# Attention's z and query scores as one product per head on 64x32 parts of TensorE's array

## The chip, the cores and the metric

The kernel runs on one core of one Trainium2 chip. The metric is the device time of one execution in microseconds (us), the median of several runs.

## The reference, cut to what matters

Two stages stand one behind the other: a "pack" attention over 8 batches of 8 heads, then two MLPs over all 4608 tokens.

```python
def sm_attn(qq, kk, vv):
    s = scale * np.matmul(qq, kk.transpose(0, 1, 3, 2))
    a = softmax(s)                       # max, exp, sum, divide
    return np.matmul(a, vv)
...
p_packed = sm_attn(p, k, v)              # 32 packed rows of 64 for each head; k, v have 576 rows
out = sm_attn(q, p_packed, p_packed)     # 576 query rows for each head
...
x = out.transpose(0, 2, 1, 3).reshape(4608, 512)
h = x @ w_in;   x = (h - tanh(h)) @ w_out            # first MLP, 512 -> 2048 -> 512
h = x @ w_in2;  x = (s * relu(h)**2 + b) @ w_out2    # second MLP, same sizes
```

The kernel never forms `out`. It multiplies the packed rows of each head with the head's 64 rows of `w_in` first, z = p_packed @ w_in (for each batch 8 heads x 32 rows by 2048 columns), and then h = z^T a2, where a2 are the 256 attention weights of a token (8 heads x 32).

## The kernel before

The program of all engines is written out in one order by hand. The main loop goes over the batches b, the two halves hf of a batch's 576 tokens (288 each), and 16 tiles j of 128 hidden columns. For each j it issues `mm1` (6 products of 128x288 into the PSUM tile `h`, L386), `act1` and `split_g` (tanh on ScalarE, the subtraction and the low part on VectorE, L394, L395, L131, L132), and `mm2` (12 products into four PSUM tiles `acc`, L409) for a tile two or three steps back.

Everything else is a generator, `fill`, that issues one small step at every call of `slot()`: `mm1` calls it once, each of `mm2`'s four groups of three products once, and the loop once more. So one step follows about three products of the main loop. `wait(n)` lets n steps pass. For each batch `fill` makes `step_p` and `stage1` (scores of p against k, softmax, product with v, the packed rows transposed into `pblk`), `make_z` for c = 0 to 3 (512 hidden columns each), and `second_stage` for the two halves, which is `stage2` (query scores, softmax, `a2`) for g = 0 and 1, four heads each, issued in turn by `both`. `more`, the conversion of the second MLP's weights through `cv` (L118 to L659), gets every third step.

A matrix `pblk[b][:, g]` holds four heads. Its 128 rows are (u, e, d): two halves u of the head dimension, two heads e of a pair, 32 dims d. Its 128 columns are the four heads' 32 packed rows. `mask` sets to zero the rows of the other head of a pair. So one product takes a pair of heads hp: contraction over all 128 rows, half of them zeros, 64 output partitions (the 64 columns of the pair):

```python
# pair_scores (L228): the query scores of group g, 288 tokens
nc.tensor.matmul(ps[hp*64:hp*64+64, :hi-lo], lhsT[:, hp*64:hp*64+64], kts[hp][:, lo:hi], ...)
# make_z (L362): z of group g, 512 hidden columns
nc.tensor.matmul(ps[g][hp*64:hp*64+64, :], pblk[b][:, g, hp*64:hp*64+64], w1[c][:, 2*g+hp, :], ...)
```

Both are float32 products; the profile has two matmul records for each of them. The trace writes their part of the array as 128\*64. `stage2` transposes a pair's q with VectorE (`qT`, L315), waits `W_Q` = 3 steps, issues the two products of its group, and VectorE transposes the scores back out of PSUM (L324). `make_z` puts group 0 and group 1 into two PSUM tiles `zp` one step apart, then ScalarE copies a tile into z (L366) and VectorE subtracts the copy for the low part (L368), group 0 first. `zp`, the score tiles and the other attention tiles share two PSUM banks (`bank_a`); `h` has two of its own (`bank_h`). SyncE issues the loads of k (L170, four transfers of 64 partitions for each group), q (L197) and w_in (L148).

Of the kernel before, what the change touches and what calls it, by code (L numbers as in the profile page):

```python
# [18 lines left out]
def pack_attention_two_mlps(ctx, tc, q, k, v, p, w_in1, w_out1, w_in2, w_out2, s_in, b_in, out):  # L19

# [51 lines left out]
    mask = apool.tile([P, 2, 2, D // 2], F32, name="mask")  # L72
# [67 lines left out]
    def load_w1(c, i):  # L140

        t = wslot(I64, f"w1s_{c}_{i}", [P, CH // 2, CW])
        rows = w_in1[i * 2 * P:(i + 1) * 2 * P, c * CW:(c + 1) * CW]
        rows = rows.rearrange("(t e u d) f -> u e d t f", e=2, u=2, d=32)
        for u in range(2):
            for e in range(2):
                p0 = (2 * u + e) * 32
                nc.sync.dma_start(out=t[p0:p0 + 32], in_=rows[u, e])  # L148
        return t
# [7 lines left out]
    k_t, v_t, q_t, pc_t, ppT, pblk, a2, z = {}, {}, {}, {}, {}, {}, {}, {}  # L157
# [3 lines left out]
    def load_k(b, g, slot=None):  # L161
        for hp in range(2):
            h0 = 4 * g + 2 * hp
            if slot is None:
                t = apool.tile([P, NB, 32], F32, tag="kr", name=f"k_{b}_{g}_{hp}", bufs=2)
            else:
                t = slot.rearrange("p a c -> p (a c)")[:, hp * S:(hp + 1) * S].rearrange("p (n m) -> p n m", m=32)
            for u in range(2):
                src = k[b, h0:h0 + 2, :, u * 32:u * 32 + 32].rearrange("e (r n) d -> (e r) n d", n=NB)
                nc.sync.dma_start(out=t[u * 64:u * 64 + 64], in_=src)  # L170
            k_t[b, g, hp] = t
# [16 lines left out]
    def load_q(b, hf):  # L188
        for g in range(G):
            for hp in range(2):  # L190
                h0 = 4 * g + 2 * hp
                t = apool.tile([P, HB // 32, 32], F32, tag="qr", name=f"q_{b}_{hf}_{g}_{hp}", bufs=4)
                for u in range(2):
                    for e in range(2):
                        src = q[b, h0 + e, hf * HB:(hf + 1) * HB, u * 32:u * 32 + 32]
                        p0 = (2 * u + e) * 32
                        nc.sync.dma_start(out=t[p0:p0 + 32], in_=src.rearrange("(n r) d -> r n d", r=32))  # L197
                q_t[b, hf, g, hp] = t
# [7 lines left out]
    def step_p(b):  # L206
        pc = pc_t.pop(b)
        pp = apool.tile([P, G, P], F32, tag="pp", name=f"pp_{b}")
        for g in range(G):
            nc.vector.tensor_tensor(  # L210
                out=pp[:, g].rearrange("p (u e d) -> p u e d", u=2, e=2),
                in0=pc[:, g].rearrange("p (u e d) -> p u e d", u=2, e=1).to_broadcast([P, 2, 2, D // 2]),
                in1=mask, op=ALU.mult)
        yield from wait(W_P)
        ps = bank_a(f"ppT_{b}")
        for g in range(G):
            nc.tensor.transpose(ps[:, g * P:(g + 1) * P], pp[:, g], ident)
        yield
        ppT[b] = apool.tile([P, G, P], F32, tag="ppT", name=f"ppT_{b}", bufs=2)
        nc.scalar.copy(ppT[b], ps[:, :G * P])  # L220
        yield
# [9 lines left out]
    def stage1(b, g, then_k=None, then_v=None, slot=None):  # L231
# [57 lines left out]
        for c in range(CT):  # L289
            n = P if c < C - CT else R  # L290
            for hp in range(2):
                nc.tensor.matmul(ps[hp * 64:hp * 64 + 64, :P], e1T[:n, c, hp * 64:hp * 64 + 64],  # L292
                                 vt[:n, 2 * hp:2 * hp + 2, c].rearrange("r e (u d) -> r u e d", u=2),
# [3 lines left out]
        if then_v:  # L297
            load_v(*then_v)
        pk = apool.tile([P, P], F32, tag="pk", name=f"pk_{b}_{g}", bufs=2)
        nc.vector.scalar_tensor_tensor(out=pk, in0=ps[:, :P], scalar=nm[:, 9:10],  # L300
                                       in1=mask.rearrange("p u e d -> p (u e d)"), op0=ALU.mult, op1=ALU.mult)
# [9 lines left out]
    def stage2(b, hf, g):  # L311
        qT = []
        for hp in range(2):
            qT.append(apool.tile([P, HB], F32, tag="qT", name=f"qT_{b}_{hf}_{g}_{hp}", bufs=4))
            nc.vector.transpose(out=qT[hp], in_=flat(q_t.pop((b, hf, g, hp))))  # L315
            yield
        yield from wait(W_Q)
        ps = bank_a(f"s2_{b}_{hf}_{g}")
        pair_scores(ps, pblk[b][:, g], qT, 0, HB)
        yield  # L320
        NBK = HB // 32
        t = apool.tile([P, NBK, M], F32, tag="t2", name=f"t2_{b}_{hf}_{g}", bufs=2)
        st = apool.tile([P, 3, NBK, 1], F32, tag="st", name=f"st_{b}_{hf}_{g}", bufs=2)
        nc.vector.transpose(out=flat(t), in_=ps[:, :HB])  # L324
        yield
# [29 lines left out]
    def make_z(b, c):  # L355
        zt = wpool.tile([P, 2, G, CW], F32R, tag="w", name=f"z_{b}_{c}")
        z[b, c] = zt
        ps = []
        for g in range(G):
            ps.append(bank_a(f"zp_{b}_{c}_{g}"))  # L360
            for hp in range(2):
                nc.tensor.matmul(ps[g][hp * 64:hp * 64 + 64, :], pblk[b][:, g, hp * 64:hp * 64 + 64],  # L362
                                 w1[c][:, 2 * g + hp, :], start=True, stop=True)
            yield
        for g in range(G):
            nc.scalar.copy(zt[:, 0, g], ps[g])  # L366
            yield
            nc.vector.tensor_tensor(out=zt[:, 1, g], in0=ps[g], in1=zt[:, 0, g].bitcast(F32), op=ALU.subtract)  # L368
            yield
# [91 lines left out]
    with tc.manual_schedule():  # L461
# [72 lines left out]
        def second_stage(b, hf):  # L534
            yield from both([stage2(b, hf, g) for g in range(G)])
            done.add(("a", b, hf))
# [39 lines left out]
        for h4 in range(4):  # L576
            nc.vector.memset(mask[h4 * M:(h4 + 1) * M, :, h4 % 2], 1.0)
# [31 lines left out]
        def second_weights():  # L609
# [23 lines left out]
            for n in range(N):  # L633
# [32 lines left out]
                if out2 and f == FT - 1:  # L666
                    ps = bank_a(f"cs_{i}")
                    for h in range(2):
                        nc.tensor.matmul(ps[:, 2 * h:2 * h + 2], csum[:, h], ones, start=True, stop=True)
                    yield  # L670
# [525 lines left out]
```

## Time and profile before

| what | value |
|---|---|
| median of 3 runs | 1614.13 us (1612.8 to 1617.1) |
| the profiled execution's own time | 1611.81 us |
| its span, first to last instruction | 1610.0 us |
| mean granted TensorE clock | 0.979 of 2.4 GHz |
| busy: TensorE, VectorE, ScalarE, GpSimd | 94%, 68%, 46%, 7% of the span |

The attention and the first MLP end at about 880 us, the second MLP fills the rest. Matmul records are pipelined: each lasts from its start to the end of its last column, so successive records overlap, and the price of a product is read from one start to the next. PEld is TensorE's weight load, DVE is VectorE, ACT is ScalarE, SPq is SyncE's queue.

### The profile page before, as it was taken

To read this page: it belongs to the slowest core of one execution; us is meant where nothing else is said; L and a number is where in the kernel's file an instruction comes from. 1 tells how busy PE (TensorE), PEld (TensorE's weight loads), DVE (VectorE), ACT (ScalarE), POOL (GpSimd) and SP (SyncE) were. 2 spreads that over 40 slices of the span, in tenths; PEclk is the share of its full clock that TensorE was granted. 3 is DMA by queue.
4 is the path that set the end of the run, shared out by engine and by line. 5 is a ranking of instruction groups with operands and counts; after the bars stand their busy time and mean duration, and the time that the engine had idled before them with its cause. 6 is when DMAs were issued, how large, how long until landed. Compare 5 with 4: busy or idle time off the path is not lost.

```text
span 1610.0 us, 26179 instructions
## 1 busy us (share of the span) xinstructions
PE 1514.9 (94%) x9592; PEld 1397.2 (87%) x9592; DVE 1091.7 (68%) x2076; ACT 745.9 (46%) x1417; POOL 109.7 (7%) x143
## 2 busy tenths in 40 slices
PE   5577999999999999999999999999998899999998
PEld 2466688888888888888799999999998899999998
DVE  5987676867768677686744677777664565565554
ACT  2344344444444444444433566566554554454452
POOL 0343100000000000000101000000011000000000
PEclk9798999999999999999999999999999999999999
DMA  9746554463544535354534754664689876786783
GB/s 193 184 107 155 124 136 117 112 153 87 140 116 124 135 100 145 97 130 111 155 116 154 295 212 181 238 244 169 228 316 396 308 224 193 225 238 183 222 256 79
DMA packets 395345, 285.65 MB, mean 177 GB/s; under 512 B 242640, under 2 KB 340944, under 8 KB 395216
## 3 DMA queue, kind: packets, MB, share of 16 engines
q1 hardware_dynamic: 386624, 254.03, 53.7%
q0 software_dynamic: 8064, 29.36, 5.0%
q8 instruction: 75, 1.23, 0.3%
q10 hardware_dynamic: 528, 0.59, 0.1%
q14 instruction: 54, 0.44, 0.1%
HBM read 168.43 MB, written 115.47 MB: 176 GB/s over the span
## 4 chain that ended last, share of the span: by engine, by line
PE 77%; DVE 10%; DMA 7%; issue 2%; SPq 2%; ACT 2%; ACTq 0%; POOL 0%; DVEq 0%; POOLq 0%
PE acc L409 20%; PE h L386 10%; PE Y L1136 9%; PE Y L921 8%; PE Z L1136 6%; PE X L1136 6%; PE X L921 5%; PE Z L921 5%; PE zp L362 3%; DMA g<-g 3%; PE s L228 2%; DMA w1s<-in_moe_w_in_dram 1%; PE pv L292 1%; DVE gl L132 1%; DVE t L395 1%
## 5 line engine op out<-in xcount | busy, mean ns | idle before, releaser
L409 PE MATMUL acc<-gh,wo 128*128 128x288 f32 x2040 | 423.2, 298 | 0.0
L409 PEld LDWEIGHTS acc<-gh,wo 128*128 128x128 f32 x2040 | 334.2, 191 | 0.0
L409 PE MATMUL acc<-gl,wo 128*128 128x288 f32 x1020 | 316.4, 310 | 5.9 <-POOL gl L132 5.5
L394 ACT ACTIVATE t<-h 128x288 f32<-128x288 f32 x256 | 105.4, 412 | 324.6 <-PE h L386 277.2
L409 PEld LDWEIGHTS acc<-gl,wo 128*128 128x128 f32 x1020 | 195.0, 191 | 55.7 <-issue 35.1
L395 DVE TENSOR_TENSOR t<-h,t 128x288 f32<-128x288 f32 x256 | 115.2, 450 | 184.7 <-ACT t L394 184.2
L386 PE MATMUL h<-a2h,z 128*128 128x288 f32 x1024 | 215.1, 298 | 3.2 <-DVE z L368 3.2
L836 DVE TENSOR_TENSOR x<-B,x 128x768 fp32r<-128x768 f32 x158 | 146.7, 950 | 87.8 <-ACT x L1070 72.4
L386 PE MATMUL h<-a2l,z 128*128 128x288 f32 x512 | 157.7, 308 | 20.6 <-DVE a2l L352 19.1
L386 PEld LDWEIGHTS h<-a2h,z 128*128 128x128 f32 x1024 | 166.3, 191 | 3.7 <-DVE z L368 3.7
L921 PE MATMUL Y<-x,w 128*128 128x384 f32 x864 | 161.1, 340 | 8.7 <-DVE g L836 7.9
L921 PEld LDWEIGHTS Y<-x,w 128*128 128x128 f32 x864 | 153.7, 191 | 9.3 <-DVE g L836 8.3
L1136 PE MATMUL Y<-x,w 128*128 128x384 f32 x864 | 153.2, 335 | 0.7 <-DVE s L836 0.7
L1136 PEld LDWEIGHTS Y<-x,w 128*128 128x128 f32 x864 | 150.3, 188 | 1.0 <-DVE s L836 1.0
L386 PEld LDWEIGHTS h<-a2l,z 128*128 128x128 f32 x512 | 97.9, 191 | 39.0 <-DVE a2l L352 20.6
L1070 ACT CAST x<-B 128x768 fp32r<-128x768 f32 x116 | 93.6, 833 | 51.0 <-DMA B<-g 30.3
L921 PE MATMUL Z<-x,w 128*128 128x384 f32 x576 | 109.9, 340 | 4.2 <-DVE u L836 4.2
L131 ACT CAST gh<-t 128x288 fp32r<-128x288 f32 x255 | 108.7, 426 | 1.1 <-DVE t L395 1.1
L921 PE MATMUL X<-x,w 128*128 128x384 f32 x576 | 108.1, 336 | 0.0
L921 PEld LDWEIGHTS Z<-x,w 128*128 128x128 f32 x576 | 102.4, 191 | 4.5 <-DVE u L836 4.5
L1136 PE MATMUL X<-x,w 128*128 128x384 f32 x576 | 102.2, 335 | 0.0
L132 DVE TENSOR_TENSOR gl<-t,gh 128x288 fp32r<-128x288 f32 x224 | 102.0, 456 | 0.0
(148 smaller groups left out, 2089.2 us busy)
## 6 DMA issues: line engine op xcount, KB each, us to landing
g<-g SPq DMA_DIRECT2D x196, 384.0 KB, 3.6
B<-g SPq DMA_DIRECT2D x116, 384.0 KB, 4.6
w<-w_d POOLq DMA_DIRECT2D x28, 512.0 KB, 6.7
w<-wo_d POOLq DMA_DIRECT2D x28, 512.0 KB, 8.0
k<-in_k_dram SPq DMA_DIRECT2D x64, 144.0 KB, 4.3
q<-in_q_dram SPq DMA_DIRECT2D x256, 36.0 KB, 2.1
B<-x2t SPq DMA_DIRECT2D x24, 384.0 KB, 5.7
g<-s SPq DMA_DIRECT2D x24, 384.0 KB, 2.6
```

The source lines that it names most:

```text
L131: nc.scalar.copy(hi, x)
L132: (eng or nc.vector).tensor_tensor(out=lo, in0=x, in1=hi.bitcast(F32), op=ALU.subtract)
L228: nc.tensor.matmul(ps[hp * 64:hp * 64 + 64, :hi - lo], lhsT[:, hp * 64:hp * 64 + 64], kts[hp][:, lo:hi], start=True, stop=True)
L362: nc.tensor.matmul(ps[g][hp * 64:hp * 64 + 64, :], pblk[b][:, g, hp * 64:hp * 64 + 64], w1[c][:, 2 * g + hp, :], start=True, stop=True)
L386: nc.tensor.matmul(h[:, :HB], zt[:, zi, g, f0:f0 + P], a[:, g], start=(n == 0), stop=(n == 3 * G - 1))
L394: nc.scalar.activation(t, h[:, :HB], AF.Tanh)
L395: nc.vector.tensor_tensor(out=t, in0=h[:, :HB], in1=t, op=ALU.subtract)
L409: nc.tensor.matmul(acc[m][:, :HB], w[:, m * P:(m + 1) * P], x, start=(j == js[0] and i == 0), stop=(j == js[-1] and i == 2))
L836: self.nc.vector.tensor_tensor(out=o, in0=a, in1=b, op=op)
L921: self.nc.tensor.matmul(bank[:, f, :self.TH], w[:, f, a, kt], x[:, b, kt], start=(p in ("P1", "P5", "P6") and m == 0), stop=(m == 5), skip ...
L1070: self.nc.scalar.copy(self.xs[(7 * self.NBK + n) % self.XS][:, 0], self.ready[0])
L1136: nc.tensor.matmul(bank[:, ft, :T], w[:, kk, u, ft], x[:, v, kk], start=first and p in ("P1", "P5", "P6"), stop=last, skip_group_check=True)
```

## The change

The rows of `pblk` are now (e, u, d) by pair: the even head of each pair has rows 0 to 63, the odd head rows 64 to 127, and q, k and w_in are loaded in that order. z and the query scores are made by one new function, `head_products`: one product per head, with contraction over its own 64 rows and 32 output partitions, so each takes a 64x32 part of the array. Head 2i+e goes to PSUM tile e, partitions 32i to 32i+31; all eight heads of a z or of a half's scores stand in succession. The new generator `scores2` transposes all four pairs of q, waits `W_Q` steps, and issues the eight products of both PSUM tiles; `stage2` begins behind that. A set `taken` makes a generator wait a step at a time until both tiles of the last user have been handed to VectorE. The mask is no longer applied to the packed rows (a `tensor_scalar` takes the place of a `scalar_tensor_tensor`), k is loaded in eight transfers of 32 partitions, and the small `cs` product of the second MLP's bias uses `bank_h`.

```diff
         t = wslot(I64, f"w1s_{c}_{i}", [P, CH // 2, CW])
-        rows = w_in1[i * 2 * P:(i + 1) * 2 * P, c * CW:(c + 1) * CW]
-        rows = rows.rearrange("(t e u d) f -> u e d t f", e=2, u=2, d=32)
-        for u in range(2):
-            for e in range(2):
-                p0 = (2 * u + e) * 32
-                nc.sync.dma_start(out=t[p0:p0 + 32], in_=rows[u, e])
+        rows = w_in1[i * 2 * P:(i + 1) * 2 * P, c * CW:(c + 1) * CW].rearrange("(t p) f -> p t f", p=P)
+        for r in range(4):
+            nc.sync.dma_start(out=t[r * 32:r * 32 + 32], in_=rows[r * 32:r * 32 + 32])
         return t
...
                 t = slot.rearrange("p a c -> p (a c)")[:, hp * S:(hp + 1) * S].rearrange("p (n m) -> p n m", m=32)
-            for u in range(2):
-                src = k[b, h0:h0 + 2, :, u * 32:u * 32 + 32].rearrange("e (r n) d -> (e r) n d", n=NB)
-                nc.sync.dma_start(out=t[u * 64:u * 64 + 64], in_=src)
+            for e in range(2):
+                for u in range(2):
+                    src = k[b, h0 + e, :, u * 32:u * 32 + 32].rearrange("(r n) d -> r n d", n=NB)
+                    p0 = (2 * e + u) * 32
+                    nc.sync.dma_start(out=t[p0:p0 + 32], in_=src)
             k_t[b, g, hp] = t
...
                         src = q[b, h0 + e, hf * HB:(hf + 1) * HB, u * 32:u * 32 + 32]
-                        p0 = (2 * u + e) * 32
+                        p0 = (2 * e + u) * 32
                         nc.sync.dma_start(out=t[p0:p0 + 32], in_=src.rearrange("(n r) d -> r n d", r=32))
...
             nc.vector.tensor_tensor(
-                out=pp[:, g].rearrange("p (u e d) -> p u e d", u=2, e=2),
-                in0=pc[:, g].rearrange("p (u e d) -> p u e d", u=2, e=1).to_broadcast([P, 2, 2, D // 2]),
+                out=pp[:, g].rearrange("p (e d) -> p e d", e=2),
+                in0=pc[:, g].rearrange("p (e d) -> p e d", e=1).to_broadcast([P, 2, D]),
                 in1=mask, op=ALU.mult)
...
                 nc.tensor.matmul(ps[hp * 64:hp * 64 + 64, :P], e1T[:n, c, hp * 64:hp * 64 + 64],
-                                 vt[:n, 2 * hp:2 * hp + 2, c].rearrange("r e (u d) -> r u e d", u=2),
+                                 vt[:n, 2 * hp:2 * hp + 2, c],
                                  start=(c == 0), stop=(c == CT - 1))
         pk = apool.tile([P, P], F32, tag="pk", name=f"pk_{b}_{g}", bufs=2)
-        nc.vector.scalar_tensor_tensor(out=pk, in0=ps[:, :P], scalar=nm[:, 9:10],
-                                       in1=mask.rearrange("p u e d -> p (u e d)"), op0=ALU.mult, op1=ALU.mult)
+        nc.vector.tensor_scalar(out=pk, in0=ps[:, :P], scalar1=nm[:, 9:10], scalar2=None, op0=ALU.mult)
         yield from wait(W_PK)
...
+
+    taken = set()
+
+    def head_products(ps, b, rhs):
+
+        for i in range(H // 2):
+            for e in range(2):
+                h, r = 2 * i + e, slice(e * D, (e + 1) * D)
+                nc.tensor.matmul(ps[e][i * M:(i + 1) * M, :rhs(i).shape[-1]],
+                                 pblk[b][r, h // 4, h % 4 * M:h % 4 * M + M], rhs(i)[r], start=True, stop=True)
+
+    def scores2(b, hf):
+        qT = []
+        for i in range(H // 2):
+            qT.append(apool.tile([P, HB], F32, tag="qT", name=f"qT_{b}_{hf}_{i}", bufs=4))
+            nc.vector.transpose(out=qT[i], in_=flat(q_t.pop((b, hf, i // 2, i % 2))))
+            yield
+        yield from wait(W_Q)
+        while taken:
+            yield
+        taken.update(("s2", e) for e in range(2))
+        sc[b, hf] = [bank_a(f"s2_{b}_{hf}_{e}") for e in range(2)]
+        head_products(sc[b, hf], b, lambda i: qT[i])
+        yield
+
     def stage2(b, hf, g):
-        qT = []
-        for hp in range(2):
-            qT.append(apool.tile([P, HB], F32, tag="qT", name=f"qT_{b}_{hf}_{g}_{hp}", bufs=4))
-            nc.vector.transpose(out=qT[hp], in_=flat(q_t.pop((b, hf, g, hp))))
-            yield
-        yield from wait(W_Q)
-        ps = bank_a(f"s2_{b}_{hf}_{g}")
-        pair_scores(ps, pblk[b][:, g], qT, 0, HB)
-        yield
+        ps = sc[b, hf][g]
         NBK = HB // 32
         nc.vector.transpose(out=flat(t), in_=ps[:, :HB])
+        taken.discard(("s2", g))
         yield
...
         z[b, c] = zt
-        ps = []
-        for g in range(G):
-            ps.append(bank_a(f"zp_{b}_{c}_{g}"))
-            for hp in range(2):
-                nc.tensor.matmul(ps[g][hp * 64:hp * 64 + 64, :], pblk[b][:, g, hp * 64:hp * 64 + 64],
-                                 w1[c][:, 2 * g + hp, :], start=True, stop=True)
-            yield
+        while taken:
+            yield
+        taken.update(("z", e) for e in range(2))
+        ps = [bank_a(f"zp_{b}_{c}_{e}") for e in range(2)]
+        head_products(ps, b, lambda i: w1[c][:, i])
+        yield
+        yield
         for g in range(G):
             nc.vector.tensor_tensor(out=zt[:, 1, g], in0=ps[g], in1=zt[:, 0, g].bitcast(F32), op=ALU.subtract)
+            taken.discard(("z", g))
             yield
...
         def second_stage(b, hf):
+            yield from scores2(b, hf)
             yield from both([stage2(b, hf, g) for g in range(G)])
...
                 if out2 and f == FT - 1:
-                    ps = bank_a(f"cs_{i}")
+                    ps = bank_h(f"cs_{i}")
                     for h in range(2):
                         nc.tensor.matmul(ps[:, 2 * h:2 * h + 2], csum[:, h], ones, start=True, stop=True)
-                    yield
                     for h in range(2):
                         nc.vector.tensor_scalar(out=bias[:, m:m + 1], in0=ps[:, 2 * h:2 * h + 1], scalar1=b_sb,
```

On TensorE, around the query scores of batch 3, half 0 (376.82 us in the trace). `acc` rows are `mm2` (`gl_2_1_7`, `gh_2_1_7` are its tile j = 7), `h` rows are `mm1`, `s` are the score tiles. Before:

```order
L386 MATMUL h_1_9_4019<-a2h_1_3267,z_2_2999 128x288 x2
L409 MATMUL acc_2_1_0_3689<-gl_2_1_7_3955,wo_6_720 128x288
L409 MATMUL acc_2_1_0_3689<-gh_2_1_7_3954,wo_6_720 128x288 x2
L409 MATMUL acc_2_1_0_3690<-gl_2_1_7_3955,wo_6_720 128x288
L409 MATMUL acc_2_1_0_3690<-gh_2_1_7_3954,wo_6_720 128x288 x2
L409 MATMUL acc_2_1_0_3691<-gl_2_1_7_3955,wo_6_720 128x288
L409 MATMUL acc_2_1_0_3691<-gh_2_1_7_3954,wo_6_720 128x288 x2
L409 MATMUL acc_2_1_0_3692<-gl_2_1_7_3955,wo_6_720 128x288
L409 MATMUL acc_2_1_0_3692<-gh_2_1_7_3954,wo_6_720 128x288 x2
L228 MATMUL s_3_0_0_4047<-qT_0_0_0_3998,pblk_3597 64x288
L228 MATMUL s_3_0_0_4047<-qT_0_0_1_4008,pblk_3597 64x288
L386 MATMUL h_1_10_4050<-a2l_1_3268,z_2_2999 128x288
```

The second group's two products follow three `h` products later. The same place after the change:

```order
L404 MATMUL h_1_9_4135<-a2h_1_3346,z_2_3066 128x288 x2
L427 MATMUL acc_2_1_0_3797<-gl_2_1_7_4067,wo_6_740 128x288
L427 MATMUL acc_2_1_0_3797<-gh_2_1_7_4066,wo_6_740 128x288 x2
L318 MATMUL s_3_0_0_4153<-qT_0_0_4114,pblk_3679 32x288
L318 MATMUL s_3_0_1_4154<-qT_0_0_4114,pblk_3679 32x288
L318 MATMUL s_3_0_0_4153<-qT_0_1_4119,pblk_3679 32x288
L318 MATMUL s_3_0_1_4154<-qT_0_1_4119,pblk_3679 32x288
L318 MATMUL s_3_0_0_4153<-qT_0_2_4124,pblk_3679 32x288
L318 MATMUL s_3_0_1_4154<-qT_0_2_4124,pblk_3679 32x288
L318 MATMUL s_3_0_0_4153<-qT_0_3_4130,pblk_3679 32x288
L318 MATMUL s_3_0_1_4154<-qT_0_3_4130,pblk_3679 32x288
L427 MATMUL acc_2_1_0_3798<-gl_2_1_7_4067,wo_6_740 128x288
```

The scores of all eight heads now stand together, and three `acc` products behind `h_1_9` instead of twelve.

On VectorE, the same place after the change: `z` is the low part of z for c = 1, `t` and `gl` belong to the main loop's tile h_1_8, `cv` to the weights' conversion.

```order
L385 TENSOR_TENSOR z_1_4071<-zp_1_0_4072,z_1_4071 128x512
L385 TENSOR_TENSOR z_1_4071<-zp_1_1_4073,z_1_4071 128x512
L413 TENSOR_TENSOR t_1_8_4106<-h_1_8_4098,t_1_8_4106 128x288
L133 TENSOR_TENSOR gl_2_1_8_4110<-t_1_7_4063,gh_2_1_8_4109 128x288
L121 TENSOR_SCALAR cv<-cv 128x512
L325 STREAM_TRANSPOSE qT_0_0_4114<-q_0_0_0_3380 128x288
L325 STREAM_TRANSPOSE qT_0_1_4119<-q_0_0_1_3385 128x288
L325 STREAM_TRANSPOSE qT_0_2_4124<-q_0_1_0_3390 128x288
L124 SCALAR_TENSOR_TENSOR cv<-w2s,cv 128x512
L325 STREAM_TRANSPOSE qT_0_3_4130<-q_0_1_1_3395 128x288
L413 TENSOR_TENSOR t_1_9_4142<-h_1_9_4135,t_1_9_4142 128x288
```

This row of operations is the same as before the change at this place. What moved is TensorE's use of the last transposed tile, from behind twelve `acc` products to behind three. Over the whole program, of the 32 z's 10 had their four products in succession before and 22 in two pairs with main-loop products between; now all 32 stand as eight in succession.

## Rows read from the trace of the kernel before

**Rows 1.** The page's head: span; busy us, share, instructions.

```profile
span 1610.0 us, 26179 instructions
PE 1514.9 (94%) x9592; PEld 1397.2 (87%) x9592; DVE 1091.7 (68%) x2076; ACT 745.9 (46%) x1417; POOL 109.7 (7%) x143
```

**Rows 2.** Busy time by stretch (clock, DMA share, GB/s at the end).

```profile
63.00:170.00 107.00, 79.92 (x497) 68.29 (x495) 87.16 (x149) 43.54 (x99) 41.38 (x35) 0.89 0.51 121
170.00:810.00 640.00, 627.49 (x4408) 535.97 (x4409) 476.11 (x1235) 280.11 (x728) 34.77 (x49) 1.00 0.49 126
```

**Rows 3.** TensorE's waits, 170 to 810 us: total, times, longest us.

```profile
PE e1Tp L272 <- ACT e L265: 3.8, 1, 3.8
```

**Rows 4.** Timeline of TensorE, half a z: start, us, record, count.

```profile
392.95 0.43 PE L386 MATMUL h<-a2h,z 128*128 128x288 f32 x2
...
393.35 0.42 PE L386 MATMUL h<-a2h,z 128*128 128x288 f32 x2
393.70 1.08 PE L362 MATMUL zp<-w,pblk 128*64 128x512 f32 x4
...
394.95 0.43 PE L409 MATMUL acc<-gh,wo 128*128 128x288 f32 x2
```

**Rows 5.** Timeline of TensorE, a z in one piece.

```profile
183.59 0.42 PE L386 MATMUL h<-a2h,z 128*128 128x288 f32 x2
183.94 1.94 PE L362 MATMUL zp<-w,pblk 128*64 128x512 f32 x8
...
186.05 0.42 PE L409 MATMUL acc<-gh,wo 128*128 128x288 f32 x2
```

**Rows 6.** Timeline of TensorE, the query scores of one group.

```profile
376.46 0.43 PE L409 MATMUL acc<-gh,wo 128*128 128x288 f32 x2
376.82 0.71 PE L228 MATMUL s<-qT,pblk 128*64 128x288 f32 x4
...
377.69 0.43 PE L386 MATMUL h<-a2h,z 128*128 128x288 f32 x2
```

**Rows 7.** Busy time by stretch, zp alone: PE, PEld, DVE, ACT (records in it).

```profile
393.69:393.72 0.03, 0.02 (x2) 0.02 (x2) 0.03 (x1) 0.00 (x0) 1.00 0.40 73
393.72:394.15 0.43, 0.43 (x2) 0.17 (x4) 0.41 (x1) 0.00 (x0) 1.00 0.49 79
```

**Rows 8.** Timeline of VectorE before the scores of rows 6.

```profile
376.14 0.47 DVE L315 STREAM_TRANSPOSE qT<-q 128x288 f32<-128x288 f32 x1
```

**Rows 9.** Timeline of VectorE, first and last of the 13 like places.

```profile
204.76 0.83 DVE L315 STREAM_TRANSPOSE qT<-q 128x288 f32<-128x288 f32 x2
...
802.47 0.82 DVE L315 STREAM_TRANSPOSE qT<-q 128x288 f32<-128x288 f32 x2
```

**Rows 10.** Timeline of TensorE at the same two places.

```profile
206.96 0.71 PE L228 MATMUL s<-qT,pblk 128*64 128x288 f32 x4
...
803.72 0.71 PE L228 MATMUL s<-qT,pblk 128*64 128x288 f32 x4
```

**Rows 11.** Tile zp, who empties it: ns min/median/max, first and last start.

```profile
L366 ACT CAST z<-zp x64: 567/587/601, 36.7 to 797.2; 128x512 fp32r<-128x512 f32 x64
L368 DVE TENSOR_TENSOR z<-zp,z x64: 645/684/693, 38.2 to 797.8; 128x512 fp32r<-128x512 f32 x64
```

**Rows 12.** The page's groups: busy us, mean ns of one, idle before.

```profile
L394 ACT ACTIVATE t<-h 128x288 f32<-128x288 f32 x256 | 105.4, 412 | 324.6 <-PE h L386 277.2
...
L132 DVE TENSOR_TENSOR gl<-t,gh 128x288 fp32r<-128x288 f32 x224 | 102.0, 456 | 0.0
```

**Rows 13.** Timeline of SyncE at the start.

```profile
1.25 3.38 SPq L170 DMA_DIRECT2D k<-in_k_dram  x4
```

**Rows 14.** The chain that ended last, before 170 us: start, us, what.

```profile
26.95 0.46 SPq L197
...
82.55 0.69 PE s L228 x4
...
97.28 1.08 PE zp L362 x4
```

More of the change, by code (lines that the diff above doesn't have):

```diff
@@ L71, in pack_attention_two_mlps @@
     ident = apool.tile([P, P], F32, name="ident")
-    mask = apool.tile([P, 2, 2, D // 2], F32, name="mask")
+    mask = apool.tile([P, 2, D], F32, name="mask")
     s_sb = const.tile([P, 1], F32, name="s_sb")
@@ L154, in split_wo @@
         yield from split_seq(t[:, 0], t[:, 1], x, eng)
-    k_t, v_t, q_t, pc_t, ppT, pblk, a2, z = {}, {}, {}, {}, {}, {}, {}, {}
+    k_t, v_t, q_t, pc_t, ppT, pblk, sc, a2, z = {}, {}, {}, {}, {}, {}, {}, {}, {}
     def load_k(b, g, slot=None):
@@ L309, in stage1, with stage2 @@
         yield
-    def stage2(b, hf, g):
+    taken = set()
[6 more added lines that the diff above has]
+    def scores2(b, hf):
         qT = []
-        for hp in range(2):
-            qT.append(apool.tile([P, HB], F32, tag="qT", name=f"qT_{b}_{hf}_{g}_{hp}", bufs=4))
-            nc.vector.transpose(out=qT[hp], in_=flat(q_t.pop((b, hf, g, hp))))
+        for i in range(H // 2):
+            qT.append(apool.tile([P, HB], F32, tag="qT", name=f"qT_{b}_{hf}_{i}", bufs=4))
+            nc.vector.transpose(out=qT[i], in_=flat(q_t.pop((b, hf, i // 2, i % 2))))
             yield
         yield from wait(W_Q)
-        ps = bank_a(f"s2_{b}_{hf}_{g}")
-        pair_scores(ps, pblk[b][:, g], qT, 0, HB)
+        while taken:
[3 more added lines that the diff above has]
+        head_products(sc[b, hf], b, lambda i: qT[i])
         yield
+    def stage2(b, hf, g):
+        ps = sc[b, hf][g]
         NBK = HB // 32
@@ L576, in pack_attention_two_mlps @@
         for h4 in range(4):
-            nc.vector.memset(mask[h4 * M:(h4 + 1) * M, :, h4 % 2], 1.0)
+            nc.vector.memset(mask[h4 * M:(h4 + 1) * M, h4 % 2], 1.0)
         run(step_p(0))
```

## The prediction

> **What bounds the kernel now.** I read the page's head first: TensorE is busy 94% of the span, VectorE 68% [rows 1]. Such a share is a mean over stages, so I cut the span. From 170 to 810 us, where 28 of the 32 z's and 14 of the 16 query-score halves are made, TensorE is busy 627.5 of 640 us at clock 1.00 (the level of 2.4 GHz), VectorE 476.1, ScalarE 280.1 [rows 2]. There TensorE sets the pace, and what is taken from it is time won unless a new wait gives it back. From 63 to 170 us neither engine is full (TensorE 79.9, VectorE 87.2 of 107) [rows 2]; there the chain of work alternates between engines, loads and queues, and a shorter product counts only where the chain runs through it.
>
> **The price of a z and of scores now.** The timeline gives it from one start to the next. Around half a z, 393.35 to 394.95 us is 1.60 us [rows 4]; it holds the four zp records and three main-loop products (two h, and one acc in the row left out). Main-loop products start about 0.131 us apart: from 392.95 to 393.35 there are three, two h of that row and one in the row left out [rows 4]. So half a z costs 1.60 - 0.39 = 1.21 us. A z in one piece, 183.59 to 186.05, costs 2.46 - 0.39 = 2.07 us [rows 5]. The second half therefore costs 0.86 us when it follows at once: two passes of 0.43 us over 512 columns, which two products of 64 columns do side by side. The remaining 0.35 us is paid once for each visit: the array falls empty before and after it. Scores of one group cost 376.46 to 377.69, 1.23 - 0.39 = 0.84 us [rows 6], that is 0.35 + two passes of 0.24.
>
> That the two 64-column products run side by side is seen by counting: two zp matmuls start within 0.03 us, and no third within the next 0.43 us, while four weight loads lie in that time [rows 7].
>
> **What is removed.** The new order puts eight products of a z, or of a half's scores, in succession, each on its own 64x32 part. If all eight run side by side as two do now, a z needs two passes: 0.35 + 0.86 + something for starting six further parts. For that the rows give two ends: two starts lie within 0.03 us, so nearly nothing, or four 64-column loads take about 0.2 us of weight-load time, 0.05 each, 0.3 for six [rows 7]. I take 0.05, since matmuls start before later loads end in these rows. So a z costs 1.26, a half's scores 0.35 + 0.48 + 0.05 = 0.88 us.
>
> From 170 to 810 us: 20 z's that stood in two halves save 2.42 - 1.26 = 1.16 each, 23.2 us; 8 in one piece save 0.81 each, 6.5; 14 score halves save 1.68 - 0.88 = 0.80 each, 11.2. Sum **40.9 us**; by the upper end of the starting price, 42 visits times 0.25, 30.4.
>
> A rule speaks against it. The Trainium skill ("TensorE: Matmul & The Clock Gate", Part 3, The mechanism) says that a weight load overlaps running matmuls only when its row group differs; the four heads of one half of the rows would then take turns. Rows 7 differ: both parts there span all 128 rows, and four loads lie beside two running matmuls. By the rows the sum is 40.9 us won, by the rule some 50 lost (third rival). No row here shows two row halves at work together. The Trainium skill ("TensorEngine Tiling (Array Packing)", Key Properties) says that tiles operate independently; no row here shows that for tiles of different rows.
>
> **What is added.** *A wait before the scores.* Before, `both` mixed the two groups' steps, so six steps lay between the last transposition of q and the first scores; now there are three. The order shows it as nine products fewer, 9 x 0.131 = 1.18 us. VectorE's own list there is the same. At batch 3 the last transposition ended at 376.61 [rows 8] and the scores began at 376.82 [rows 6], 0.21 us later; nine products earlier TensorE waits 0.97 us, 1.02 with 0.05 for the signal. Over the 13 like places from 205.59/206.96 to 803.29/803.72 us [rows 9, 10] that distance runs from -0.23 to 1.37 us, mean 0.76; place by place the waits sum to **6.3 us** (0 to 1.5 each). Everything on TensorE queues behind it, first the main loop.
>
> *A wait before z, c = 3.* Both PSUM tiles are now taken at once, 30 products after c = 2 took them: 5.2 us from start to start. The second tile's subtraction stands behind tanh, t, gl and one cv of tile h_14, whose products end 3.0 us after the start: tanh 0.41, three VectorE operations of some 0.45, then its own 0.68 [rows 11, 12], ready near 5.5. 0.3 us at six batches: **2 us**. *Batch 1*, where c = 1 follows c = 0 by 18 products and scores follow by 9: two ScalarE copies of 0.59 and a subtraction of 0.68 in a row [rows 11] reach past the 1.2 us of the nine products by about 1 us, so twice 1: **2 us**. *cs on the h banks* (twice): between nothing and one more turn of tanh and t, about 1 us each; I take **1 us** in all. Waits of this size leave the clock alone: a wait of 3.8 us [rows 3] lies in the stretch whose clock is 1.00 [rows 2].
>
> *Loads of k.* Four transfers took SyncE 3.38 us at the start [rows 13]; eight of half the size cost between 0.46 (a q transfer, a quarter of the size, L197) [rows 14] and 0.85 each, 3.7 to 6.8 us; near the lower, 4.4, so 1 us later on the chain that runs through SyncE there, and 1 us more for batch 1's k. Against it, before 170 us: the chain passes through scores at 82.55 and a z half at 97.28 [rows 14], and both get shorter, by about 0.5 and 1.2 us. I take these **together as nothing**, within 3 us either way: VectorE's conversions and the loads cover the rest there, and without that cover four z's would add 4 us of gain.
>
> *Nothing:* the packed rows' scaling loses an operand on VectorE, off TensorE's path; w_in and q change rows, not transfers; the order of softmax steps moves by a few steps, under VectorE's 164 us of slack in the stretch.
>
> **Sum.** 40.9 - 6.3 - 2 - 2 - 1 = 29.6 us. The profiled execution took 1611.8 us (span 1610.0), so 1582.2; the median of the runs lies 2.3 us above that execution: **1585 us**.
>
> **The rivals.**
> *Half as much side by side.* Four columns' streams of moving data, or the two row halves, take turns, so each visit needs four passes. A z costs 0.35 + 1.72 + 0.05 = 2.12, scores 0.35 + 0.96 + 0.05 = 1.36: 20 x 0.30 - 8 x 0.05 + 14 x 0.32 = 10.1 us won, since halves no longer pay 0.35 twice. The scores come 0.48 us later, so waits shrink to about 5. **1609 us**, at the edge of what can be told from no change. For: rows 7 show two streams, never four, and never two row halves. Against: two streams cost each other nothing.
>
> *Waits eat the gain.* If each of the 13 scores waits as long as the worst above (1.5 us, 19 in all), z for c = 3 and batch 1 double to 8, and each remaining z waits 0.3 for a tile, 6: 33 us of waits, 8 won, about **1606 us**. It decides from about 1 us of wait at each of the 42 visits. For: VectorE has 476 us of work for what would be 610 us. Against: it is in step with TensorE's h tiles, so its lag does not pile up.
>
> *Slower: the four heads of one row half take turns* (the rule above). Eight passes to a visit: a z costs 0.35 + 8 x 0.43 = 3.79, scores 0.35 + 8 x 0.24 = 2.27. Lost: 20 x 1.37 + 8 x 1.72 + 14 x 0.59 = 49.4 us: **1663 us**. It decides from five passes to a visit on. Against it stand rows 7.
>
> **How the numbers follow.** Forecast 0.70 (alone 1574 to 1596: 41 won with few waits, or starting at 0.3 and somewhat longer waits), half 0.14, waits 0.08, slower 0.07. The range 1571 to 1609 holds the forecast, the waits case and half of the second, about 0.85 of the chance, and ends below at all of the gain with no wait and 2 of the start's 3 us. About 0.3%, 4.8 us, is what a measurement here tells from no change. Faster: forecast, waits and half of "half", 0.85; same 0.07; slower 0.08.
>
> **What would show it.** In the profile after: zp records in the form 64\*32, 16 to a z, lying in 1.1 to 1.3 us from first start to last end (1.9 or more: half; 3.5: turns). Scores in 0.75. TensorE's busy time from 170 us to the end of the first MLP's attention down by about 40 us, and in the list of waits a new row, scores on qT, of 5 to 8 us, at 13 places. The forecast is wrong if the parts do not run together, or if the waits on qT and z exceed 20 us.

## The result, and the profile after

The changed kernel took 1594.12 us (median of 4 runs, 1592.67 to 1598.22), the kernel before 1614.58 us on the same chip: ratio 0.9876, 95% interval 0.9853 to 0.9900. That is 20 us won, where 29 were forecast. The profiled execution of the changed kernel took 1598.22 us, the longest of its four, and that of before 1611.81, so their spans differ by only 13.5 us. The page's head and the windows of [rows 1, 2], for the changed kernel:

```profile
span 1596.5 us, 27039 instructions
...
PE 1483.3 (93%) x9976; PEld 1389.4 (87%) x9976; DVE 1088.6 (68%) x2076; ACT 743.0 (47%) x1417; POOL 108.4 (7%) x143
```

```profile
63.00:170.00 107.00, 72.02 (x480) 62.34 (x479) 84.20 (x136) 44.30 (x100) 40.94 (x36) 0.87 0.51 123
170.00:810.00 640.00, 623.51 (x4919) 552.10 (x4918) 491.20 (x1279) 284.78 (x748) 37.51 (x52) 0.99 0.52 132
```

From 170 to 810 us TensorE is as busy as before, because more work now lies in that stretch. From 63 to 170 us it does less than before, 72.0 against 79.9 us: the program comes into that stretch late.

**The price of a visit.** TensorE's timeline around a z and around a half's scores where nothing is waited for:

```profile
393.51 0.43 PE L427 MATMUL acc<-gh,wo 128*128 128x288 f32 x2
393.87 1.09 PE L318 MATMUL zp<-w,pblk 64*32 64x512 f32 x16
394.88 0.40 PE L427 MATMUL acc<-gl,wo 128*128 128x288 f32 x1
395.12 0.42 PE L427 MATMUL acc<-gh,wo 128*128 128x288 f32 x2
...
788.75 0.43 PE L427 MATMUL acc<-gh,wo 128*128 128x288 f32 x2
789.11 0.72 PE L318 MATMUL s<-qT,pblk 64*32 64x288 f32 x16
789.75 0.40 PE L427 MATMUL acc<-gl,wo 128*128 128x288 f32 x1
789.99 0.42 PE L427 MATMUL acc<-gh,wo 128*128 128x288 f32 x2
```

Read as before, 395.12 - 393.51 = 1.61 us less three main-loop products of 0.13: a whole z costs **1.22 us** (forecast 1.26; before 2.42 or 2.07). Scores cost 1.24 - 0.39 = **0.85 us** (forecast 0.88; before 1.68). The windows of the zp records alone show why:

```profile
393.86:393.90 0.04, 0.03 (x6) 0.04 (x8) 0.00 (x0) 0.00 (x0) 1.00 0.00 0
393.90:394.30 0.40, 0.40 (x8) 0.14 (x16) 0.00 (x0) 0.00 (x0) 1.00 0.00 0
```

Six matmuls have begun within 0.04 us of the first, and through the next 0.40 us eight stand side by side, with sixteen weight loads in the same time. In [rows 7] there were two, with four.

**Where the rest went.** Two landmarks cut the span: the first z product of batch 1, and the last `h` product of the attention. Before they stand at 179.48 and 877.13 us, after at 190.20 and 862.90. So the stretch between them fell from 697.65 to 672.70 us, **25.0 us won**, and the start grew by **10.7 us** in this execution. A second profile of the same kernel, below, has 187.43 and 672.11.

*In the stretch* the 42 visits hold more waiting than was forecast. Each visit's price less 1.22 or 0.85 us, summed over all, is 10.6 us at the scores and 8.8 us at the z's. Much of it lies within a visit, whose first products have begun. The worst scores, and a z of c = 3; first TensorE, then VectorE between the last two z's:

```profile
492.64 0.42 PE L404 MATMUL h<-a2h,z 128*128 128x288 f32 x2
493.00 1.04 PE L318 MATMUL zp<-w,pblk 64*32 64x512 f32 x2
494.38 1.09 PE L318 MATMUL zp<-w,pblk 64*32 64x512 f32 x14 [0.35 <-DVE z L385]
495.40 0.40 PE L427 MATMUL acc<-gl,wo 128*128 128x288 f32 x1
```

```profile
311.42 0.48 DVE L325 STREAM_TRANSPOSE qT<-q 128x288 f32<-128x288 f32 x1 [1.32 <-DMA q<-in_q_dram]
...
492.22 0.68 DVE L385 TENSOR_TENSOR z<-zp,z 128x512 fp32r<-128x512 f32 x1
492.82 0.45 DVE L413 TENSOR_TENSOR t<-h,t 128x288 f32<-128x288 f32 x1
493.19 0.45 DVE L133 TENSOR_TENSOR gl<-t,gh 128x288 fp32r<-128x288 f32 x1
493.55 0.68 DVE L385 TENSOR_TENSOR z<-zp,z 128x512 fp32r<-128x512 f32 x1
```

The z of c = 3 puts one product into its first PSUM tile at 493.00 and the next at 494.38: the second tile is given free by the last row, which ends at 494.23 and stood behind t and gl. Such a visit costs 2.6 us. The worst scores began at 308.95 and waited 2.96 us for the transposition at 311.42, whose q landed late.

*At the start* the chain that ended last passes through the second converted half of w_in (L127 on VectorE) into the z of c = 3, as it did before, but there with the first half:

```profile
133.31 0.99 issue
134.30 1.82 DVE w L127
...
136.16 1.59 PE zp L318 x8
137.75 2.83 PE acc L427 x12
```

Before, the like rows are w L126 at 126.06 for 1.14 us, the half z at 127.33 and acc x12 in 1.83 us. Two things are in this difference. The first converted half is done near 134.4, and the z's first eight records start at 134.53, but the other eight wait until 136.16 for the second half. And the end of the z and the twelve acc products ran at a lower granted clock: 0.60 from 137.6 to 140.6 us, where it was 1.00 for the like products of the kernel before. From the start of the first w row to the end of the acc products it is 7.3 us (7.7 in the second profile), and 4.2 before. And SyncE's queue at the start:

```profile
1.25 5.44 SPq L170 DMA_DIRECT2D k<-in_k_dram  x8
6.73 2.03 SPq L146 DMA_DIRECT2D w1s<-in_moe_w_in_dram  x4
8.80 7.21 SPq L170 DMA_DIRECT2D k<-in_k_dram  x8
```

Before, beside [rows 13], the second group of k:

```profile
6.85 6.17 SPq L170 DMA_DIRECT2D k<-in_k_dram  x4
```

Eight transfers of k took 5.44 us where four took 3.38, and the second eight 7.21 where four took 6.17: 3.1 us more in all.

### The profile page after: what moved, and what is told of

The parts are those of the page before. It is cut to its first block, busy times and chain, and to the rows that moved or that the text cites. A ratio compares the mean times of both kernels' runs of the same rounds, so it can differ in the third digit from the quotient of the medians.

```text
span 1596.5 us, 27039 instructions
## 1 busy us (share of the span) xinstructions
PE 1483.3 (93%) x9976; PEld 1389.4 (87%) x9976; DVE 1088.6 (68%) x2076; ACT 743.0 (47%) x1417; POOL 108.4 (7%) x143
## 4 chain that ended last, share of the span: by engine, by line
PE 72%; DVE 10%; DMA 8%; SPq 4%; issue 3%; ACT 2%; DVEq 0%; ACTq 0%
PE acc L427 19%; PE Y L1154 9%; PE h L404 9%; PE Y L939 8%; PE Z L1154 6%; PE X L1154 6%; PE X L939 5%; PE Z L939 5%; DMA g<-g 3%; PE zp L318 2%; SPq L197 1%; DMA q<-in_q_dram 1%; DVE gl L133 1%; DMA w1s<-in_moe_w_in_dram 1%; PE pv L292 1%
## 5 line engine op out<-in xcount | busy, mean ns | idle before, releaser
L939 PE MATMUL Z<-x,w 128*128 128x384 f32 x576 | 109.6, 339 | 4.4 <-DVE u L854 4.4
L1154 PE MATMUL Z<-x,w 128*128 128x384 f32 x576 | 102.0, 335 | 0.0
```

Source lines behind the costliest of these rows:

```text
L939: self.nc.tensor.matmul(bank[:, f, :self.TH], w[:, f, a, kt], x[:, b, kt], start=(p in ("P1", "P5", "P6") and m == 0), stop=(m == 5), skip ...
L1154: nc.tensor.matmul(bank[:, ft, :T], w[:, kk, u, ft], x[:, v, kk], start=first and p in ("P1", "P5", "P6"), stop=last, skip_group_check=True)
```

## The experiments

The theory: all eight products of a visit run side by side, which is worth some 42 us; it is given back by (1) the doubled transfers of k on SyncE, (2) batch 0's z's, which now need both converted halves of w_in, (3) scores that wait for the last qT, and (4) z's that wait for a PSUM tile. The rivals: the late start has another cause or varies by itself, and a wait that is covered in one place comes back in another. All runs in one table; "first z" is that of batch 1, "stretch" from there to the attention's last `h` product, "waits" the sum over the 42 visits.

| kernel | median us | ratio to before (95%) | first z | stretch | waits |
|---|---|---|---|---|---|
| before | 1612.84 to 1614.58 | 1 | 179.48 | 697.65 | |
| after | 1594.12 | 0.9876 (0.9853 to 0.9900) | 190.20 | 672.70 | 19.4 |
| after, again | 1593.29 | 0.9874 (0.9857 to 0.9891) | 187.43 | 672.11 | 18.7 |
| before, k in eight | 1617.14 | 1.0027 (1.0015 to 1.0038) | 184.68 | 697.58 | |
| half of batch 0's k from ScalarE | 1593.74 | 0.9884 (0.9869 to 0.9899) | 184.56 | 672.27 | |
| batch 0's z in two groups | 1590.42 | 0.9866 (0.9851 to 0.9880) | 181.28 | 674.18 | 19.5 |
| six steps before scores | 1594.22 | 0.9885 (0.9872 to 0.9899) | 186.64 | 672.84 | 19.9 |
| c = 3 later | 1602.29 | 0.9927 (0.9915 to 0.9940) | 188.99 | 678.29 | 19.1 |
| row halves in two visits | 1632.57 | 1.0117 (1.0101 to 1.0133) | 186.96 | 708.45 | |
| four edits | 1584.44 | 0.9815 (0.9800 to 0.9831) | 187.09 | 661.55 | 2.9 |
| steps and split z | 1581.73 | 0.9804 (0.9791 to 0.9818) | 183.10 | 664.33 | 2.9 |
| the same, k from ScalarE | 1578.32 | 0.9782 (0.9769 to 0.9796) | 179.81 | 664.27 | 3.0 |

**After, again.** No edit.

> The changed kernel once more, unaltered. Theory: from the first z of batch 1 on, an execution takes 1406.4 us to its end, as in the first profile, and what differs between executions lies before it (184 to 190 us); so span minus the start of that z is 1406.4 within 0.5 us, and the median of the times is 1592 to 1595. Rival (the waits behind the start vary from one execution to the next): the stretch behind that z differs by more than 1 us.

The time came as expected, but the theory of a fixed stretch fell and its rival was right: span less first z was 1403.9, where the first profile has 1406.3. Of the 2.4 us 0.6 lie in the stretch and 1.8 behind the attention, where the second MLP's two long waits, at 1207 and 1232 us in the first profile, were shorter: from one TensorE start to the next 3.7 in place of 4.7 us, and 7.4 in place of 8.5. Up to the last `h` product the two agree to 0.6 us, so the stretch is a finer measure than the time. The start varies more, by 2.8 us here.

**Both row halves at once?** The even heads' products, and a step later the odd heads'.

```diff
-        head_products(ps, b, lambda i: w1[c][:, i])
+        head_products(ps, b, lambda i: w1[c][:, i], 0)
         yield
+        head_products(ps, b, lambda i: w1[c][:, i], 1)
```

> The changed kernel with the products of the even heads (rows 0 to 63) and of the odd heads (rows 64 to 127) in two visits one step apart, four products side by side in each. Theory (both row halves work at the same time as four column blocks, and the gain needs both): each visit costs 1.2 us for z and 0.84 for scores, so a z costs 2.4 and a half's scores 1.7, and the stretch from the first z of batch 1 to the end rises from 1406 by 30 to 45 us to 1436 to 1450 (the waits get shorter), so the time is near the kernel before or above it. Rival (the four columns alone make the gain, the row halves take turns inside a visit): splitting costs only the 0.35 us of a further visit, 42 times, so the stretch rises by 15 us to about 1421.

The stretch rose by 35.8 us to 708.45, span less first z to 1440.7: the theory's 1436 to 1450. A visit of four products costs as much as one of eight. TensorE's timeline:

```profile
400.29 0.43 PE L430 MATMUL acc<-gh,wo 128*128 128x288 f32 x2
400.65 1.06 PE L318 MATMUL zp<-w,pblk 64*32 64x512 f32 x8
401.65 0.40 PE L430 MATMUL acc<-gl,wo 128*128 128x288 f32 x1
401.88 0.43 PE L430 MATMUL acc<-gh,wo 128*128 128x288 f32 x2
```

1.59 - 0.39 = 1.20 us. So the odd heads, in the other 64 rows, cost next to nothing when they come along, and the gain is the parallel work of both row halves as much as that of the columns.

**k in eight transfers, in the kernel before.**

```diff
-                src = k[b, h0:h0 + 2, :, u * 32:u * 32 + 32].rearrange("e (r n) d -> (e r) n d", n=NB)
-                nc.sync.dma_start(out=t[u * 64:u * 64 + 64], in_=src)
+                for e in range(2):
+                    src = k[b, h0 + e, :, u * 32:u * 32 + 32].rearrange("(r n) d -> r n d", n=NB)
+                    nc.sync.dma_start(out=t[(2 * u + e) * 32:(2 * u + e) * 32 + 32], in_=src)
```

> The kernel before, with nothing changed but the loads of k: eight transfers of 32 partitions for each group in place of four of 64. Theory (the start of the changed kernel is late mainly because SyncE issues twice as many transfers of k): the last k transfer of batch 0 is issued about 3 us later, q's behind it too, the first z of batch 1 starts 3 to 6 us later than 179.5 us, and the time rises by about the same, 3 to 6 us. Rival (the late start comes from the new order of z and scores, not from k): the first z of batch 1 stays within 1 us of 179.5 and the time within 2 us of the kernel before.

4.3 us slower (interval 2.4 to 6.1), the first z 5.2 us later, the stretch unchanged to 0.1 us: the theory. Of the 5.2 us in the profile, 2.7 stand already at the first z of batch 0 (32.85 against 30.17 us). Some 1.5 more come at its half z of c = 3 and the acc products behind, at a granted clock of 0.50 and 0.71 where the kernel before had 1.00; so not all of it is SyncE's time. The transfers carry the same bytes; SyncE's queue pays for their number:

```profile
1.25 5.43 SPq L172 DMA_DIRECT2D k<-in_k_dram  x8
...
8.79 7.38 SPq L172 DMA_DIRECT2D k<-in_k_dram  x8
```

**k from two queues.** The changed kernel, with this line in `load_k`:

```diff
-                    nc.sync.dma_start(out=t[p0:p0 + 32], in_=src)
+                    (nc.scalar if b == 0 and u else nc.sync).dma_start(out=t[p0:p0 + 32], in_=src)
```

> The changed kernel, with half of batch 0's k transfers issued from ScalarE's queue, the other half from SyncE's. Theory: k's and q's transfers of batch 0 are issued about 3 us earlier, the first z of batch 1 starts 2 to 5 us before 190.2, and the time falls by 2 to 5 us. Rival (the loads of k are hidden, the order of z and scores makes the late start): within 1.5 us of the changed kernel.

By the time no gain can be told, as the rival has it, though in its profile the first packed rows are transposed 2.7 us earlier and the first z stands 3 to 6 us earlier than in the two profiles of the changed kernel. The pair at the end of this section settles it.

**Batch 0's z's in two groups of pairs.**

```diff
+        if b == 0:
+            head_products(ps, b, lambda i: w1[c][:, i], (0, 1))
+            yield
+            head_products(ps, b, lambda i: w1[c][:, i], (2, 3))
+            yield
+        else:
             head_products(ps, b, lambda i: w1[c][:, i])
+            yield
+            yield
```

> The changed kernel, with the eight products of each z of batch 0 in two groups of four, pairs 0 and 1 first, pairs 2 and 3 one step later, so that the first four need only the first converted half of the weights. Theory (the eight products of batch 0's z wait for the second converted half of w_in, which the first group of the kernel before did not need): the z's of batch 0 start up to 2 us earlier each, the first z of batch 1 starts 2 to 5 us before 190.2, the time falls by 2 to 5 us. Rival (the loads in front decide, the products only follow): no gain, and four further visits of TensorE at 0.35 us, so 0 to 1.5 us slower.

The first z came at 181.28, 6 to 9 us earlier; the ratio fell by 0.1%, well within the intervals, so the time alone does not settle it. The chain shows the mechanism: the z goes in with the first converted half, and the main loop behind it runs at the pace that it had before the change. The stretch is 1.5 to 2 us longer than the changed kernel's; the granted clock was 0.50 from 304.5 to 307.5 us, where the two profiles of the changed kernel have 1.00.

```profile
129.49 1.15 DVE w L127
...
130.77 1.06 PE zp L318 x8
131.83 1.80 PE acc L433 x12
```

From the start of the w row to the end of the acc products it is 4.1 us, where the changed kernel has 7.3 and 7.7. How much of that is the wait and how much the clock, the next run tells.

**Six steps before the scores, and c = 3 later.** `W_Q` = 6 in place of 3 in one; in the other:

```diff
         def make_zs(b, c):
             while (b - 1, 1, c) not in mm1_done:
                 yield
+            if c == NCH - 1:
+                yield from wait(4)
             yield from make_z(b, c)
```

> The changed kernel with six steps in place of three between the last transposition of q and the scores. Theory (10.6 us of TensorE's waits from 185 to 800 us are scores waiting for the last transposed q, and they end when nine more main-loop products lie between): those waits fall below 2 us and the time falls by 6 to 10 us. Rival (waits only move: the softmax steps behind come later and the a2 tiles or z wait instead): the waits on q fall but the time changes by less than 3 us.

> The changed kernel with the z of c = 3 four steps later. Theory (z's of c = 3 cost 0.5 to 1.7 us too much at seven places because the second PSUM tile is given free late by VectorE, and twelve products in front of them cover that): they cost 1.2 us each, the stretch from the first z of batch 1 to the end falls from 1406.4 to 1399 to 1402. Rival (the wait moves to what stands behind): the c = 3 z's get cheap but scores or the first main-loop products of z's users wait longer, and the stretch stays within 1.5 us.

Both theories fell, and the rival of the first was right; that of the second had the mechanism, but not the size (within 1.5 us). Six steps clear the scores (10.6 us of waiting become 2.2), and the z's take it over (8.8 become 17.8): c = 3 stands later behind them and is due with the next batch's c = 0. A z of c = 3, and the list of TensorE's waits in the stretch:

```profile
681.45 1.89 PE L318 MATMUL zp<-w,pblk 64*32 64x512 f32 x16 [1.43 <-DVE z L385]
```

```profile
PE s L228 <- DVE kT L246: 5.5, 6, 1.9
PE zp L318 <- DVE z L385: 5.0, 7, 1.4
```

The pack's scores wait longer for kT, too, 5.5 us where the changed kernel has 2.9. At the start this run has a z in one piece, with the granted clock at 1.00 behind it:

```profile
132.25 1.82 DVE w L127
...
134.12 1.06 PE zp L318 x8
135.18 1.82 PE acc L427 x12
```

Its first w row starts at 131.19, so this is 5.8 us, 1.7 more than with the z split. The wait for the second half is worth 1.7 us, then, and the lower clock made the other 1.5 and 1.8 us in the two profiles of the changed kernel. Of the five profiles with a z in one piece four have a granted clock of 0.60 to 0.66 over these twelve acc products; of the six with a z in two groups of pairs (the kernel before and k in eight among them) five have 1.00. Why it is so was not tested.

With c = 3 later its visits cost 1.22 us, apart from batch 1's, and the scores behind them, now only a few steps behind the transpositions, wait up to 2.2 us more. The visits hold 19.1 us of waiting, as before, and the pack's steps wait longer: in the list of waits kT rises from 2.9 to 4.2 us, pp from 1.8 to 3.6, and gl from GpSimd is new with 1.9. Behind this last wait the granted clock was 0.57 from 207 to 211 us. So the stretch is 5.6 us longer.

**Four edits together.** Half of k from ScalarE's queue for batches 0 and 1, the split z of batch 0, `W_Q` = 6, and four steps before the z's of c = 0 and c = 3 from batch 1 on.

> The changed kernel with half of the k transfers of batches 0 and 1 issued from ScalarE's queue, batch 0's z products in two groups of pairs, six steps before the scores, and four steps more before the z's of c = 0 and c = 3 from batch 1 on. Theory (the four losses are separate and each can be covered): first z of batch 1 at 179 to 183 us, the stretch behind it 1394 to 1400, time 1576 to 1584. Rival (a batch has no steps to spare, later z's and scores push the softmax steps against the main loop's need of a2 and z): the stretch behind stays at 1404 or above, the time 1586 to 1592.

The waits in the visits fell from 19.4 to 2.9 us and the stretch by 11.1; the rest of it came back on the pack's steps (pkT on pk 4.1 us, from nothing). The start missed, 187.09. The chain shows why: batch 1's k now stands in ScalarE's queue behind its work on the weights, and SyncE's first transfer of q follows when it has landed. Not all is k: this run also puts batch 1's z of c = 0, the landmark itself, four steps later. The packed rows in front of it were transposed at 184.84 us, 2.25 before it, where the last run below has 179.55 and 0.26. So by these two profiles late k cost 5.3 us, and 2 us of the start's loss, and of the stretch's gain, are the landmark's own shift.

```profile
145.44 1.70 DVE wo1s L127
...
147.16 0.57 ACT wo L136
...
147.77 0.64 ACTq L170
...
149.14 3.31 DMA k<-in_k_dram
...
152.47 0.31 SPq L197
```

**Steps and split z, without and with k from ScalarE for batch 0 alone.** The extra steps for c = 0 from batch 2 on.

> The changed kernel with batch 0's z products in two groups of pairs, six steps before the scores, and four steps more before the z's of c = 3 (from batch 1 on) and c = 0 (from batch 2 on); k as the change has it, all from SyncE. Theory (in the version that did all this, half of batch 1's k came late from ScalarE's queue and held the chain by some 6 us): first z of batch 1 at 179 to 183 us, from there to the last main-loop product of the attention 661 to 663 us (672.7 in the changed kernel), time 1576 to 1581. Rival (what made that version's start late is the extra steps, not ScalarE's queue): first z of batch 1 at 186 us or later, time 1583 or above.

> The same with half of batch 0's k transfers, and no others, issued from ScalarE's queue. Theory (batch 0's k costs SyncE about 2.5 us on the chain that starts the program, and ScalarE is idle then): first z of batch 1 and the time 2 to 3 us before those of its sister kernel. Rival (the chain later runs through SyncE's queue of loads for batch 1 and through weights that arrive at their own pace, so an earlier k is only waited with): within 1 us of it.

The rival of the first is out as a whole (first z at 183.10), but this run also dropped batch 1's steps at c = 0, and these are 2 of the 4 us between the two starts. Its time and stretch came 1 to 2 us above the forecast: TensorE waited 1.9 us for gl from GpSimd, the granted clock was 0.50 from 201 to 204 us, and the twelve acc products there took 3.25 us in place of some 1.8. With it as a base, k's second queue is worth 3.4 us: 1578.32 (1577.65 to 1578.97) against 1581.73 (1581.23 to 1584.6). That is the best version: 35 us below the kernel before, 15 below the change. Its queue and its waits from 180 to 800 us:

```profile
1.25 2.77 SPq L170 DMA_DIRECT2D k<-in_k_dram  x4
...
8.82 3.71 SPq L170 DMA_DIRECT2D k<-in_k_dram  x4
```

```profile
PE pkT L303 <- DVE pk L300: 4.1, 5, 0.8
PE ppT L217 <- DVE pp L210: 3.3, 5, 0.9
PE acc L433 <- POOL gl L133: 1.9, 1, 1.9
```

No wait on qT is left in the list, and on a z's tile one of 0.4 us.

## Why the prediction was right, and where its sizes were off

**What is removed: right.** A z was forecast at 1.26 and scores at 0.88 us; they cost 1.22 and 0.85. With these prices the sum forecast as 40.9 is 20 x 1.20 + 8 x 0.85 + 14 x 0.83 = 42.4 us. The rival of half side by side asked for 2.12 and 1.36 and is out; so is the one of turns. The rule of the Trainium skill ("TensorE: Matmul & The Clock Gate", Part 3, The mechanism), by which a weight load overlaps running matmuls only in another row group, does not hold here: sixteen loads lie beside eight running matmuls that use all 128 rows. The tiles' independence ("TensorEngine Tiling (Array Packing)", Key Properties) does, for both row halves, by the two-visits run.

**Scores on qT: right in kind, 6.3 forecast, 9.4 measured** at the 13 places (the fourteenth, in batch 1, has 1.2). The step took the distance between transposition and scores from the places of before, less nine products. The worst, 3.0 us at 308.95, waited for q's transfer, which the step left out; the twelve others hold 6.4, where 6.0 were forecast.

**z of c = 3 and batch 1: 4 forecast, 10 measured.** The step put VectorE's tail at four operations and 0.3 us of wait at six batches; c = 3 waited 0.1 to 1.7 us at seven, 6.8 in all, and one c = 0 another 1.1. VectorE had further work of the softmax and of `cv` in front (a2l at 490.42 in the batch shown). Batch 1's scores and first two z's held 1.8 us, where 2 were forecast. The term for cs was not measured by itself; TensorE's waits of h for t in the stretch are 1.5 us before and 1.6 after, so nothing of it shows.

So the waits measured 19.4 us where 11.3 were forecast. 42.4 - 19.4 is 23.0; the stretch gained 25.0. Of the 2 us between, the kernel before held about 1 as waits in its own visits (a z at 356.70 cost 0.5 too much, one half at 794.46 0.3), and the pack's wait on pp fell from 3.3 to 1.8 us.

**Waits and the clock: misread.** The step said that waits of such a size leave the clock alone, by one wait of 3.8 us in a stretch whose mean clock is 1.00. The mean over 640 us hid that the granted clock was 0.50 from 173 to 176 us, straight behind that wait. In the changed kernel's stretch, with waits of up to 3.0 us, it was 1.00 all the same, so the sum there did not suffer; the start did, as the next step has it.

**Start and batch 0: this step failed.** It put them at nothing, within 3 us. In the profiles the first z came 8 and 11 us later; by the medians, 20.5 us gained in all against 25.0 in the stretch, 4.5 us were lost. Two parts failed. The price of k was taken near its lower end, 4.4 us for eight transfers; they took 5.4, the second group took 1.0 more, too, and alone they cost the kernel before 4.3 us. And batch 0's z was counted as a gain of 1.2 us on the chain, without the wait: a z in one piece needs both converted halves of w_in, the half z that it replaces needed one. At c = 3 that made 1.7 us, and with the lower clock 3.1 to 3.5. What the second part costs in the time alone is not settled: the split by itself shows it only in the profile. With the steps as well, the time fell by 11.3 us by the ratios to before, of which the stretch has 8. Taken together, 1.5 us more removed and the 2 not forecast, against 8.1 more of waits and 4.5 at the start, make the 9 us between 29.6 and 20.5.

**Waits eat the gain** as a rival was true in part: of its 33 us of waits there were 19. c = 3 and batch 1 came as it had them (8.6 against 8 us), the scores at half (9.4 against 19), and the remaining z's hold 1.4 of its 6. Neither of the two steps against the waits helped alone.

## What to carry to other kernels

When products are merged into one visit, price the visit from start to start, and then list for each operand when its *last* part is ready and for each PSUM tile when its last reader is done: the merged visit waits for the latest of all. Cover waits that hang on one in-order engine together: here either edit alone moved them, at no gain or at a loss, and both together gained 8 us of the stretch. Count the transfers that a new layout needs, on the queue that issues them, at the start above all.

## What the runs showed of the hardware

Eight float32 products on 64x32 parts ran side by side at the price of four: a visit of 4 and one of 8 cost 1.20 and 1.22 us, and six matmuls had started within 0.04 us. A k transfer of half the size took SyncE four fifths of the time to issue: at the median of batch 0's 632 ns for 72 KB, 788 ns for 144 KB. By the sums, 12.65 us for sixteen and 9.55 for eight, it is two thirds. A transfer on ScalarE's queue waits for the work ahead of it on that engine: with half of batch 0's k there, issued from 0.74 to 7.5 us, the program gained 3.4 us; with half of batch 1's, issued at 147 us behind a copy of weights, the start lost 5.3 us. The clock was low in the late start. In the second profile of the changed kernel TensorE waited 3.5 us for gl until 126.10, and from 128 us on the granted clock was 0.50, the lower of the two levels (1.2 of 2.4 GHz). So it had fallen before TensorE's wait of 2.3 us for w_in, which ended at 131.97, and it rose within the twelve acc products behind the z:

```profile
131.50:139.00 7.50, 7.03 (x35) 3.96 (x36) 3.53 (x6) 0.94 (x3) 0.97 (x1) 0.59 0.01 2
139.00:150.00 11.00, 8.03 (x58) 7.57 (x57) 10.05 (x17) 6.17 (x14) 5.61 (x5) 1.00 0.69 158
```
